# A two-branch layer (state-space scan beside dilated local attention) on one core: attention in natural token order

## The chip, the cores and the metric

One core of one Trainium2 chip runs the whole kernel. Times are device microseconds of one execution; the lower, the better. The core has five engines with an instruction stream each: PE (matrix products into PSUM), ACT and DVE (elementwise work and copies), POOL (small setup work) and SP (it only issues transfers). Transfers run on 16 DMA engines that SP and ACT feed through their queues.

## The reference

Two branches, each on its own x of 2048 tokens by 448, give 448 columns of the output each.

```
A: h[t] = Lam_bar * h[t-1] + B_bar @ x[t]          448 complex states, 2048 steps
   y[t] = 2 * Re(C @ h[t]) + x[t] * Dskip
B: q, k, v = split(x @ wqkv)                        16 heads of 28
   logits[t, w] = q[t] . k[t - 2w] * 28**-0.5       w = 0..7, masked where t - 2w < 0
   o[t] = sum_w softmax(logits)[t, w] * v[t - 2w]
   out_b = o @ wo
out = concat(y, out_b)                              bf16
```

## The kernel before

**Order of the work.** Python code describes the kernel as some 600 units (`Planner.add`), each with its engine, a cost, what it depends on and the buffers it takes. A list written out in the file, ORDER, then says in which order the units are emitted; each engine executes its share strictly in that order. So an instruction that waits holds everything behind it on its engine, and a transfer that waits holds SP. PSUM has two double banks (W) and four single ones (s).

**Branch B.** Token t = 16p + j lies in partition p, column group j. SP loads x transposed, one transfer per j (L348), and the weights of q, k and v (L326, L327). Projections (L466, L473, L499) give q and k transposed (channels on the partitions, qT, q3, kT, k3), a block of 8 j at a time, the upper block first. Logits: DVE multiplies q with k shifted by 2w tokens (`qk`, L639 to L645, 37 instructions in all), and PE sums each head's 28 channels with a selection matrix (L656, L662). Softmax (`softmax`, L684 to L716): maximum on DVE, exponential on ACT, sum on PE, reciprocal and normalising on DVE, transposes on PE, so that the weights lie with tokens on the partitions. V is projected for all 16 j (L741, four matmuls each) into `vd`, whose 14 leading slots are a halo: the slots of the previous partition. `halo` fills it by transfers inside the chip that shift by one partition, each cut in two, 112 partitions (L755) and 15 (L756); partition 0 is zeroed by POOL (L760). PV (`pv`): DVE multiplies weights and V (L797) and adds (L800, L809, L812), 3584 elements each; every group of four j adds to its own accumulator. The sums are transposed, for three of four groups by a transfer (L837), for the last on PE (L849), multiplied with wo (L866) and written out (L876).

**Branch A.** Parameters are turned into powers of Lam_bar on POOL and ACT (`setup`, its inputs loaded at L906 and transposed on PE at L988) and into small diagonal matrices on DVE (`powers`, L1146). The states go in seven groups m of 64 complex ones. For each, `scan` forms the input products (L1192, L1200), then a chain of PE products and ACT copies (eP L1205, e L1213, eG L1220, four steps through pbuf L1229 and L1234, h L1243, L1258, L1274); three groups are in flight. To finish a group its first values are added again with identity matmuls (L1252, L1263). `outputs` multiplies h with C (L1356) after adding x * Dskip by diagonal matmuls (L1353, six of eight pairs) or on DVE (L1367), copies (L1365) and writes out (L1370).

**The issue order on SP before the scan:** x of B, B matrices, x of A (L943, 16 transposes), halo, wo, C (L969, L973).

The lines of `halo` at issue:

```
def halo(i0, i1):
    f = lambda a, b, p0, p1: self.vd[p0:p1, a:b].rearrange("p j d h -> p (j d h)")
    s0, s1 = i0 + T, i1 + T
    nc.sync.dma_start(f(i0, i1, 1, 113), f(s0, s1, 0, 112))
    nc.sync.dma_start(f(i0, i1, 113, 128), f(s0, s1, 112, 127))
```

Of the kernel before, what the change touches and what calls it, by code (L numbers as in the profile page):

```python
# [9 lines left out]
ACT = mybir.ActivationFunctionType  # L10
# [18 lines left out]
TJ = HALO + T  # L29
# [3 lines left out]
JB = 8  # L33
QW = 2 + NCH
KPOW = [1, 2, 4, 8, 12, 16, 32, 48, 64, 128, 192, 256, 512, 768, 1024]
# [4 lines left out]
WARM = 4  # L40
FILL = (1, 3)
PRI = dict(bm=-5.66, xa=2.77, cc=19.9, sc=2.9, ch=-27.35, bk=-0.56, v0=16.0, v1=-26.16, wo=-13.74, y=14.16, pw=-5.68, sm=13.48, lim=100.0, lim2=30.0, limv=70.0, qk=0.86, K11=-14.0, Q11=-13.0, K10=-12.0, Q10=-11.0, K01=-10.0, Q01=-9.0, K00=-8.0, Q00=-7.0, d3=10.94, h0=-1.0, g0=-1.0, h1=-1.0, g1=-1.0, h2=-1.0, g2=-1.0, h3=1.0, g3=-1.0, h4=-1.0, g4=-1.0, h5=-1.0, g5=-1.0, h6=1.0, g6=1.0, nd=4.0, xd=20.12)
ORDER = [
# [51 lines left out]
class Unit:  # L95
    __slots__ = ("eng", "cost", "fn", "deps", "prio", "acq", "rel", "lat", "end", "seq", "on", "until", "mode")


class Planner:


    def __init__(self, bufs):
        self.units = []
        self.free = {k: [0.0] * n for k, n in bufs.items()}

    def add(self, eng, cost, fn, deps=(), prio=0.0, acq=None, rel=None, lat=None, until=None,
            mode="f"):
        u = Unit()
        u.mode = mode
        u.eng = eng if isinstance(eng, tuple) else (eng,)  # L110
        u.cost = cost if isinstance(cost, tuple) else (cost,)
        u.fn, u.prio, u.rel, u.until = fn, prio, rel, until
        u.acq = () if acq is None else (acq,) if isinstance(acq, str) else acq
# [4 lines left out]
        return u  # L118

    def run(self):  # L120
        left = list(self.units)
        nwait = {id(u): len({id(d) for d in u.deps}) for u in left}
        users = {}
        for u in left:
            for d in {id(d): d for d in u.deps}.values():
                users.setdefault(id(d), []).append(u)
        ready = [u for u in left if not nwait[id(u)]]
        clock = {}
        order = []
        n = len(left)  # L130
        mode = "f"
        while len(order) < n:
            best = None
            for u in ready:
                if any(len(self.free[a]) < u.acq.count(a) for a in u.acq):
                    continue
                for eng, cost in zip(u.eng, u.cost):
# [3 lines left out]
                    for a in u.acq:  # L141
                        t = max(t, sorted(self.free[a])[u.acq.count(a) - 1])
                    if u.until is not None and eng == u.eng[-1] and t > u.until:
                        continue
                    key = (t, u.prio, u.seq, t)
                    if best is None or key < best[0]:
                        best = (key, u, eng, cost + (0.095 if eng == "PE" and u.mode != mode else 0.0))
            assert best, "no unit can start: %d left, waiting for %s" % (n - len(order), [(u.acq, u.fn.__qualname__) for u in ready])
            (_, _, _, t), u, eng, cost = best
            for a in u.acq:  # L150
                self.free[a].remove(min(self.free[a]))
# [5 lines left out]
            for a in (u.rel,) if isinstance(u.rel, str) else u.rel or ():  # L157
                self.free[a].append(u.end)
# [5 lines left out]
            order.append((t, u, cost))  # L164
        self.order = order
        if len(ORDER) == n:
            for i in ORDER:
                u = self.units[i % 1000]
                u.on = u.eng[i // 1000]
                order.append((0.0, u, 0.0))  # L170
            order = order[n:]
        for _, u, _ in order:
            if len(u.eng) > 1:
                u.fn(u.on)
            else:
                u.fn()
# [15 lines left out]
class Ctx:  # L192
# [22 lines left out]
    def double(self, n, out, in_, deps, prio):  # L215

        return self.plan.add(("ACT", "DVE"), (act(n), vec2(n)), lambda eng: self.copy(eng, out, in_), deps, prio)
# [16 lines left out]
    def consts2(self):  # L234
# [19 lines left out]
        mrow = pool.tile([NCH, 4], bf16, name="mrow")  # L254
        mcol = pool.tile([NCH, 2, 2, NCH], bf16, name="mcol", tag="late_a")

        def masks():
            G.memset(mrow[:], 0.0)
            G.affine_select(out=mrow[:], in_=mrow[:], compare_op=ALU.not_equal, fill=-1e9,
                            base=-3, pattern=[[1, 4]], channel_multiplier=1)  # L260
            G.memset(mcol[:], 1.0)
            for b in range(2):
                for k in range(2):
                    v = mcol[:, b, k].rearrange("p (i r h) -> p i r h", i=4, r=2)
                    G.affine_select(out=v, in_=v, compare_op=ALU.is_ge, fill=0.0, base=8 * k - 8 * b - 1,
                                    pattern=[[-1, 4], [-4, 2], [0, H]], channel_multiplier=2)
        self.u_mask = self.plan.add("POOL", 2.7, masks, [self.boot], 1)

        def mask(b, lg):

            for k in range(2):
                nc.tensor.matmul(lg[:, 4 * k:4 * k + 4, 0], lhsT=mcol[:, b, 1 - k, :], rhs=mrow[:],
# [3 lines left out]
    def warm(self):  # L276

        nc, P = self.nc, self.plan
        self.pr = self.pool.tile([NCH, 3 * 4096], bf16, name="prods")
# [1207 lines left out]
```

## Time and profile before

| | |
|---|---|
| three runs | 141.4, 141.7, 141.99 us, median 141.7 |
| profiled execution, first to last instruction | 140.4 us |
| PE busy | 134.9 us in 1078 matmuls |
| DVE busy | 120.9 us in 128 instructions |
| ACT busy | 93.6 us in 182 instructions |
| granted clock of PE | 1.000 |
| DMA | 39390 packets, 15.99 MB |
| first q.k product on DVE | 15.48 us (half a unit), 21.98 us (the next) |
| last PV addition ends, last DVE instruction ends | 131.3 us, 137.9 us |

A row of groups reads: line, engine, operation, output<-inputs, sizes, count | busy us, mean ns of one | idle time before it and who ended it. A row of the order of time reads: start us, length us, engine, line, what. A row of the stage table reads: start:end, length, then busy us and count of PE, weight loads, DVE, ACT and POOL, then the granted clock, the mean busy share of the 16 DMA engines, and GB/s. "SPq" and "ACTq" are the issuing of transfers, whose data move later. The ends of matmuls are modelled, so two overlapping rows of PE give the pace by their starts.

### The profile page before, as it was taken

The numbers are of one execution on the slowest core, as the hardware profiler recorded it, in microseconds if no ns is written. First come the engines' busy times: TensorE is split into PE (matmuls) and PEld (weight loads), VectorE is DVE, ScalarE is ACT, GpSimd is POOL, SyncE is SP. The second block draws the span as 40 slices with busy tenths as digits, with TensorE's granted clock in tenths as the row PEclk, the third lists the DMA queues.
The fourth block names the chain that finished last, engine by engine and source line by source line (L and its number), as shares of the span: only waits on it lengthen the run. The fifth ranks groups of instructions, "written<-read, shape, count | busy, mean of one in ns | idle before, by whom it ended". The sixth has DMA issues, their size and how long they took to land.

```text
span 140.4 us, 2813 instructions
## 1 busy us (share of the span) xinstructions
PE 134.9 (96%) x1078; PEld 71.6 (51%) x1078; DVE 120.9 (86%) x128; ACT 93.6 (67%) x182; POOL 21.1 (15%) x68
## 2 busy tenths in 40 slices
PE   5999999999999999999999999999999999999990
PEld 1634333456554454666435554456655555555650
DVE  3245959999999989897998999999999999999931
ACT  3358879999765883578776789889873630551381
POOL 7374287000970000000000000000000000000000
PEclk9999999999999999999999999999999999999999
DMA  4965243996537616469999400600154155724044
GB/s 129 267 120 111 56 100 56 238 218 123 81 67 76 103 42 203 110 94 175 248 199 142 144 0 5 131 0 0 35 101 132 47 181 139 170 80 139 0 161 133
DMA packets 39390, 15.99 MB, mean 114 GB/s; under 512 B 31445, under 2 KB 38740, under 8 KB 39377
## 3 DMA queue, kind: packets, MB, share of 16 engines
q1 hardware_dynamic: 39314, 15.82, 50.6%
q8 instruction: 8, 0.13, 0.4%
q14 instruction: 5, 0.04, 0.1%
q10 hardware_dynamic: 63, 0.01, 0.0%
HBM read 4.27 MB, written 3.67 MB: 57 GB/s over the span
## 4 chain that ended last, share of the span: by engine, by line
PE 94%; DMA 2%; ACT 1%; issue 0%; DVE 0%; ACTq 0%
PE y_ps L1356 15%; PE qk_ps L466 12%; PE v_ps L741 9%; PE wo_ps L866 9%; PE scb L1192 7%; PE scP L1192 7%; PE logits L656 4%; PE scb L1234 3%; PE qk_ps L499 3%; PE qk_ps L473 2%; DMA ra<-in_B_x_dram 2%; PE scb L1209 2%; PE y_ps L1353 2%; PE scP L1200 2%; PE scP L1263 2%; PE pt_x L413 1%
## 5 line engine op out<-in xcount | busy, mean ns | idle before, releaser
L797 DVE TENSOR_TENSOR prods<-attn,vd 128x3584 bf16<-128x3584 bf16 x12 | 24.0, 2020 | 0.0
L641 DVE TENSOR_TENSOR prods<-qk 128x3072 bf16<-128x3072 bf16 (+1 forms) x17 | 22.8, 1379 | 1.0 <-PE logits L656 0.5
L800 DVE TENSOR_TENSOR rb<-rb,prods 128x3584 bf16<-128x3584 bf16 x11 | 22.2, 2022 | 0.1
L466 PE MATMUL qk_ps<-rb 128*128 128x512 bf16 x60 | 15.3, 386 | 0.0
L1356 PE MATMUL y_ps<-Ccat,qk 128*128 128x448 bf16 x64 | 14.9, 352 | 0.0
L866 PE MATMUL wo_ps<-wo_p,rb 128*128 128x448 bf16 x64 | 13.5, 352 | 0.0
L741 PE MATMUL v_ps<-rb 128*128 128x448 bf16 x64 | 13.1, 352 | 0.0
L1229 ACT CAST pbuf<-scb 128x128 bf16<-128x128 f32 x35 | 9.2, 272 | 4.9 <-PE scb L1234 4.3
L1192 PEld LDWEIGHTS <-Bcat 128*128 128x128 bf16 x84 | 7.6, 98 | 8.2 <-issue 1.9
L1356 PE MATMUL y_ps<-Ccat,h 128*128 128x448 bf16 x48 | 11.7, 353 | 0.0
L1365 ACT CAST qk<-y_ps 128x896 bf16<-128x896 f32 x6 | 5.4, 907 | 9.1 <-PE y_ps L1356 9.1
L201 ACT CAST qk<-wo_ps 128x448 bf16<-128x448 f32 (+1 forms) x16 | 8.3, 526 | 4.2 <-PE wo_ps L866 3.9
L1192 PE MATMUL scb<-xaT_sb,Bcat 128*128 128x512 bf16 x42 | 11.1, 380 | 0.0
L1192 PE MATMUL scP<-xaT_sb,Bcat 128*128 128x512 bf16 x42 | 10.9, 379 | 0.0
L201 ACT CAST qk<-qk_ps 128x512 bf16<-128x512 f32 (+2 forms) x14 | 7.8, 580 | 2.9 <-PE qk_ps L473 1.2
L203 ACT ACTIVATE qk<-qk_ps 128x512 bf16<-128x512 f32 (+1 forms) x16 | 9.3, 599 | 0.5 <-PE qk_ps L499 0.2
L466 PEld LDWEIGHTS <-rb 128*128 128x128 bf16 x60 | 5.8, 100 | 7.4 <-issue 1.2
L201 ACT CAST vd<-v_ps 128x448 bf16<-128x448 f32 x16 | 7.9, 542 | 2.5 <-PE v_ps L741 2.5
L1356 PEld LDWEIGHTS <-qk 128*128 128x128 bf16 x64 | 6.3, 98 | 5.8
L645 DVE TENSOR_TENSOR prods<-qk 128x768 bf16<-128x768 bf16 (+3 forms) x18 | 9.1, 569 | 0.1
L741 PEld LDWEIGHTS <-rb 128*128 128x128 bf16 x64 | 6.1, 98 | 5.3
L866 PEld LDWEIGHTS <-rb 128*128 128x128 bf16 x64 | 6.1, 98 | 5.0
(177 smaller groups left out, 251.9 us busy)
## 6 DMA issues: line engine op xcount, KB each, us to landing
out_dram<-qk SPq DMA_DIRECT2D x18, 112.0 KB, 1.7
out_dram<-qk SPq DMA_DIRECT2D x7, 224.0 KB, 2.2
vd<-vd SPq DMA_DIRECT2D x3, 392.0 KB
rb<-in_B_wqkv_dram SPq DMA_DIRECT2D x3, 336.0 KB
qk<-in_A_x_dram SPq DMA_DIRECT2D x1, 448.0 KB
ra<-in_A_B_re_dram SPq DMA_DIRECT2D x1, 392.0 KB
ra<-in_A_B_im_dram SPq DMA_DIRECT2D x1, 392.0 KB
rb<-in_A_C_re_dram SPq DMA_DIRECT2D x4, 98.0 KB
```

The source lines that it names most:

```text
L201: nc.scalar.copy(out, in_)
L203: nc.scalar.mul(out, in_, scale)
L466: nc.tensor.matmul(out(n), lhsT=w(n, full, k), rhs=self.xT[:, j:j + 4, k, :], start=(not rfirst and k == 1), stop=(rfirst and k == KT - 1) ...
L641: V.tensor_tensor(out.rearrange("p i j k q -> p i (j k) q"), qq.unsqueeze(1).to_broadcast([NCH, 2, 4 * nk, NCH]), bass.AP(kk.tensor, kk.of ...
L645: V.tensor_tensor(jk(out[:, i, a:e]), qq, kk, op=ALU.mult)
L741: nc.tensor.matmul(ps[:].rearrange("p h d -> p (h d)"), lhsT=self.xT[:, j, k, :], rhs=self.wv[:, k, :], start=(k == 0), stop=(k == KT - 1))
L797: V.tensor_tensor(tmp[i].rearrange("p (j d h) -> p j d h", j=8, d=DH), aa, self.vd[:, o:o + 8], op=ALU.mult)
L800: V.tensor_tensor(acc, acc, tmp[i], op=ALU.add)
L866: nc.tensor.matmul(ps[:], lhsT=o[:, kt, :], rhs=self.wo_p[:, KT * e + kt, :], start=(kt == 0), stop=(kt == KT - 1))
L1192: mt(box[i], lhsT=self.Bcat[:, k, m, :], rhs=self.xk(slice(i, None, 4), k), start=(i % 2 == 0 and k == 0), stop=False, **kw)
L1229: nc.scalar.copy(pb[:, dst, PAD:], box[3][:, 384:512])
L1356: nc.tensor.matmul(ps, lhsT=self.h[m][:, i, g * NCH:(g + 1) * NCH], rhs=self.Ccat[:, m, :], start=(m == 0 and not skip), stop=(m == NM - 1 ...
```

## The change

- **Tokens.** Branch B works on two halves of 1024 tokens, t = 1024b + 8p + j, first half first. x comes as pairs of tokens, 896 channels in seven blocks of 128: eight transposing transfers instead of thirteen. The q and k weights are loaded by ACT's queue, ahead of the parameters of branch A, in an even and an odd layout of seven blocks (the middle one is shared, half each).
- **Matmuls.** Each projection of q, k and V is three full matmuls and one half-row matmul per token of the pair; the two half-row ones are emitted together and work on different halves of PE's rows. The scan's loading is unchanged in this.
- **q.k products.** q and k lie in token order, so one instruction of 4096 elements covers four shifts of one half: 7 per half, 14 in all. k3 and q3 get their second copy by two transfers on SP. The sums in PE have 512 columns instead of 256.
- **Softmax.** The reciprocal is a logarithm and an exponential on ACT. The transposed weights go to DRAM and come back in the order in which V lies (`away`, `move`); then ACT or DVE turns them (`turn`).
- **V and PV.** Each half has its own V buffer of 22 slots, 14 of them halo. A shift by one partition is one transfer of 127 partitions, a shift by two one of 126; the second half also fetches the first half's last partitions. PV uses instructions of 7168 elements: two products and one addition per group of four j, then folds.
- **Scan.** The steps through pbuf are five on 64 columns instead of four on 128. The first values are put back by ACT copies into PSUM instead of identity matmuls, except where the bank is held (groups 3 and 6). h of groups 3 to 6 lies where the first half's V was; ACT's copy of it waits for the last PV product of that half.
- **Skip.** x is loaded again in token order over its transposed copy once the scan's input products are done, multiplied by Dskip on DVE (four instructions of 1792), and copied by ACT into PSUM before the y matmuls.
- Eight warm-up matmuls stand before the first projection instead of four; the ORDER list is a new one, and a second list names the PSUM banks.

```diff
-            nc.sync.dma_start(f(i0, i1, 1, 113), f(s0, s1, 0, 112))
-            nc.sync.dma_start(f(i0, i1, 113, 128), f(s0, s1, 112, 127))
...
+            def halo(i0, i1, b=b):
+                n = 2 if i0 < HALO - JB else 1
+                s0 = i0 + JB * n
+                nc.sync.dma_start(flat(b, n, NCH, i0, i1), flat(b, 0, NCH - n, s0, s0 + i1 - i0))
+                if b:
+                    nc.sync.dma_start(flat(1, 0, n, i0, i1), flat(0, NCH - n, NCH, s0, s0 + i1 - i0))
+            for i0, i1 in ((6, 10), (10, 14), (0, 6)):
...
+        def away():
+            d = box["d"] = cx.dram.tile([8, NCH, NCH], bf16, name="attn_d%d" % b)
+            nc.sync.dma_start(d[:].rearrange("g q e -> q g e"), self.at)
+
+        def move():
+            nc.sync.dma_start(self.at, box["d"][:].rearrange("g (p j) e -> (g p) j e", j=JB))
...
+                    V.tensor_tensor(p, q[:, t0:t0 + HB].unsqueeze(1).to_broadcast([NCH, 4, HB]),
+                                    bass.AP(k.tensor, k.offset, [k.ap[0], [DIL, 4], [1, HB]]), op=ALU.mult)
...
+                def rr(mm=mm):
+                    mm(0, lo, 3)
+                    mm(1, hi, 3)
...
+                if eng == "ACT":
+                    nc.scalar.copy(box[1], box["e1"][:])
...
-                for k in range(KT if skip and m0 == 0 else 0):
-                    n = min(NCH, D - k * NCH)
-                    nc.tensor.matmul(ps[:, k * NCH:k * NCH + n], lhsT=self.xk(j + jj, k), rhs=self.Dg[:, k, 0:n],
-                                     start=(k == 0), stop=False, skip_group_check=True)
...
+            def seed(j=j, jb=jb):
+                jb["y"] = self.psum.tile([NCH, 2, 512], f32, name="y_ps", slot=jb["s"])
+                nc.scalar.copy(jb["y"][:, :, 0:D], self.xd[j])
...
-    b.qk(1, PRI["qk"])
-    b.qk(0, PRI["qk"] + 1)
...
+    b.qk(0, PRI["qk"])
+    b.qk(1, PRI["qk"] + 1)
```

The instructions of the changed kernel around the halo stand on SP in this order: the 16 transposes of branch A's x, the second copies of k3 and q3, halo slots 6 to 9 (127 partitions), the wo loads, slots 10 to 13 (127), the skip row, `away` of the first half, slots 0 to 5 (126), `move` of the first half, slots 6 to 9 of the second half, and later, behind C's loads and the second half's `away`, its slots 0 to 5, its slots 10 to 13, `move` and C's transpose.

More of the change, by code (lines that the diff above doesn't have):

```diff
@@ L215, in double @@
     def double(self, n, out, in_, deps, prio):
-        return self.plan.add(("ACT", "DVE"), (act(n), vec2(n)), lambda eng: self.copy(eng, out, in_), deps, prio)
+        return self.plan.add(("ACT", "DVE"), (act(n) + 0.04, vec2(n)), lambda eng: self.copy(eng, out, in_), deps, prio)
     def consts(self):
@@ L286, in mm @@
             if first:
-                box["ps"] = self.psum.tile([NCH, 2, 512], f32, name="warm_ps", tag="W")
+                box["ps"] = self.psum.tile([NCH, 2, 512], f32, name="warm_ps", slot=self.warm_slot)
             for _ in range(n):
@@ L648, in summ @@
                     if head:
-                        self.lg[b] = self.psum.tile([NCH, W, NCH], f32, name="logits", tag="W")
+                        self.lg[b] = self.psum.tile([NCH, W, NCH], f32, name="logits", slot=self.lg_slot[b])
                     lg, pr = self.lg[b], ub["pr"]
-                    new = tp // 2 not in begun
-                    begun.add(tp // 2)
-                    zs = slice(H - H * par, 3 * H - H * par)
-                    for kt in range(3):
-                        for i in range(4):
-                            nc.tensor.matmul(lg[32 * i:32 * i + 32, 2 * tp:2 * tp + 2, :],
-                                             lhsT=cx.Z[:, kt, zs], rhs=pr[:, :, i, kt, :],
-                                             start=(new and kt == 0), stop=(kt == 2), skip_group_check=True)
@@ L727, in v_proj @@
+        u = P.add("PE", pe(8, 128), tr, [u], -1, acq=s_at, rel="at")
+        u = P.add("ACT", act(1024), ev, [u, *self.u_attn.get(0, ())], -1, rel=s_at)
+        u = P.add("SP", 0.6, away, [u], -1, lat=2.3)
+        u = P.add("SP", 0.6, move, [u], -1, lat=2.3)
+        self.u_attn[b] = [P.add(("ACT", "DVE"), (act(512), vec2(512)), lambda eng, r=r: turn(eng, r), [u], -1) for r in range(2)]
     def v_proj(self, prio, deps):
-        nc, pool, P, cx = self.nc, self.pool, self.plan, self.cx
+        nc, P, cx = self.nc, self.plan, self.cx
@@ L839, in pv @@
-        for j in range(j0, j0 + JB):
-            jb = {}
-            g = j // 4
-            def tr(j=j, jb=jb):
-                pt = jb["pt"] = self.psum.tile([NCH, KT, NCH], f32, name="pt_o", tag="s")
+                    o = (3584, 6272, 8064)[g]
+                    t = self.oTd[g] = rb[:, o:o + n1].rearrange("p (k q) -> p k q", q=NCH)
+                    nc.sync.dma_start(t, res[g], transpose=True)
+                trs[r] = self.u_trd[g] = P.add("SP", 2.5, trd, [lasts[r][1], *self.u_vm], PRI["wo"], lat=2.0)
@@ L845, in tr @@
+        for j in range(JB):
+            jb, st, sl = {}, Slot("s", 2), Slot("s", 1)
+            g = 2 * b + j // 4
+            def tr(j=j, jb=jb, st=st):
+                pt = jb["pt"] = self.psum.tile([NCH, KT, NCH], f32, name="pt_o", slot=st)
                 a = j % 4 * D
@@ L1260, in back @@
-            def back(box=box):
-                box["P"] = self.psum.tile([NCH, 2, 512], f32, name="scP", tag="W")
-                for i in range(2):
-                    mt(box["P"][:, i, :], lhsT=cx.ident[:], rhs=box["eP"][:, i, :], start=True, stop=False, **kw)
-            def s6(box=box, pb=pb, L=L, hget=hget):
-                carry(box["P"][:, 0, :], L(1), pb, hget())
-            def s7(box=box, L=L, hget=hget):
-                mt(box["P"][:, 1, :], lhsT=L(1), rhs=hget()[:, 1, :], start=False, stop=True, **kw)
@@ new lines, in s5, with ev1f @@
+            def s5(box=box, L=L, hget=hget, carry=carry, sl=sl, m1=m1):
+                if m1 == "add":
+                    box[1] = self.psum.tile([NCH, 512], f32, name="scb1", slot=sl["b1"])[:]
+                carry(box[1], L(2), hget(), m1 == "add")
+            def ev1f(eng, box=box, hget=hget, m1=m1):
+                if m1 == "add":
+                    nc.vector.tensor_tensor(hget()[:, 1, :], box[1], box["e1"][:], op=ALU.add)
+                else:
+                    cx.copy(eng, hget()[:, 1, :], box[1])
@@ new lines, in back, with p2 @@
+            def back(eng, box=box, sl=sl, mP=mP):
+                box["P"] = self.psum.tile([NCH, 2, 512], f32, name="scP", slot=sl["P2"])
+                if eng == "ACT":
+                    nc.scalar.copy(box["P"][:], box["eP"][:])
+                else:
+                    for i in range(2):
+                        mt(box["P"][:, i, :], lhsT=cx.ident[:], rhs=box["eP"][:, i, :], start=True, stop=False, **kw)
+            def p2(box=box, sl=sl, mP=mP):
+                if mP == "add" and "P2" not in box:
+                    box["P"] = box["P2"] = self.psum.tile([NCH, 2, 512], f32, name="scP", slot=sl["P2"])
+                return box["P"]
@@ L1396 @@
+                P.add("SP", 0.1, lambda f=out: f(j0=1, j1=2), [v, o], pr, rel="ya", lat=2.0)
 @with_exitstack
```

1108 lines of the change are left out of this document (487 added, 621 removed), and 59 rows, old and new, of tables (BANKS, ORDER).

## Prediction

> **What bounds the kernel now.** I read the page's busy shares and its chain first, then busy time by stage, then the groups by shape, then the order of time on each queue.
>
> ```profile
> span 140.4 us, 2813 instructions
> PE 134.9 (96%) x1078; PEld 71.6 (51%) x1078; DVE 120.9 (86%) x128; ACT 93.6 (67%) x182; POOL 21.1 (15%) x68
> ...
> PE 94%; DMA 2%; ACT 1%; issue 0%; DVE 0%; ACTq 0%
> ```
> ```profile
> 20.00:25.00 5.00, 5.00 (x24) 2.06 (x23) 4.52 (x6) 4.37 (x9) 3.80 (x8) 1.00 0.33 66
> ...
> 80.00:90.00 10.00, 10.00 (x70) 5.11 (x67) 9.93 (x7) 8.95 (x20) 0.00 (x0) 1.00 0.24 46
> ...
> 120.00:130.00 10.00, 10.00 (x61) 5.34 (x60) 9.96 (x6) 3.57 (x6) 0.00 (x0) 1.00 0.43 123
> ```
> In the stage rows (length, then busy us of PE, PEld, DVE, ACT, POOL, then clock, DMA share, GB/s) PE is full throughout and DVE is full from about 22 us on. The chain names PE, but shortening PE alone would not carry far: DVE stands right beside it. So the new time is the later of two chains: DVE (first q.k product, then DVE's work and its waits, then a tail) and the scan on ACT and PE with the y products behind it.
>
> **PE: about 6 us less.** The pace of a matmul is read from the chain.
> ```profile
> 34.90 3.78 PE v_ps L741 x20
> ...
> 90.53 0.32 PE scP L1200 x2
> 90.85 0.22 PE scb L1200 x2
> ...
> 131.44 0.89 PE pt_o L849 x16
> ```
> ```profile
> L1353 PE MATMUL y_ps<-Dg,xaT_sb 128*128 128x128 bf16 (+1 forms) x48 | 4.3, 212 | 0.0
> ...
> L1263 PE MATMUL scP<-eP,ident 128*128 128x512 bf16 x10 | 3.0, 378 | 0.0
> ...
> L1252 PE MATMUL scb<-e,ident 128*128 128x512 bf16 x6 | 2.3, 378 | 0.0
> ```
> 448 columns take 0.189 us, 128 take 0.056; a pair of half-row matmuls runs side by side in 0.22, plus 0.1 to enter that mode. Gone are the 48 skip matmuls (about 48 x 0.055 = 2.6) and the 16 identity matmuls (16 x 0.22 = 3.5). V goes from 64 full matmuls to 48 and 8 pairs: 8 x 0.189 = 1.5 less, 8 x 2 x 0.1 = 1.6 more. The projections go from 88 and 12 pairs to 98 of 512 columns, the logits keep their columns: 0.4 less, nothing. The scan's middle goes from 10 to 11 narrower matmuls per group: nothing. Sum about -6.5 us.
>
> **ACT: about 20 us more, not the bound by itself.**
> ```profile
> L1229 ACT CAST pbuf<-scb 128x128 bf16<-128x128 f32 x35 | 9.2, 272 | 4.9 <-PE scb L1234 4.3 <-PE scb L1226 0.2
> ...
> L1205 ACT CAST eP<-scP 128x1024 bf16<-128x1024 f32 x7 | 7.2, 1028 | 1.5 <-PE scP L1200 1.4
> ...
> L1213 ACT CAST e<-scb 128x512 bf16<-128x512 f32 x7 | 4.2, 595 | 2.4 <-PE scb L1209 2.4
> ```
> ACT now writes PSUM before the matmuls add to it: 5 x 1.03 and 6 x 0.6 in the scan, 8 x 0.91 before y, 16.3 in all, and one more short copy per group, 7 x 0.27. A write of ACT into PSUM is not in this trace: between nothing extra and twice the eviction of that size, I take the eviction's time. 93.6 + 18 + a few evictions is under 115.
>
> **DVE: about the same work, begun 7 us earlier.**
> ```profile
> L797 DVE TENSOR_TENSOR prods<-attn,vd 128x3584 bf16<-128x3584 bf16 x12 | 24.0, 2020 | 0.0
> L800 DVE TENSOR_TENSOR rb<-rb,prods 128x3584 bf16<-128x3584 bf16 x11 | 22.2, 2022 | 0.1
> L641 DVE TENSOR_TENSOR prods<-qk 128x3072 bf16<-128x3072 bf16 x11 | 19.2, 1757 | 1.0 <-PE logits L656 0.5 <-ACT vd L201 0.2
> ```
> ```profile
> 21.98 1.76 DVE L641 TENSOR_TENSOR prods<-qk 128x3072 bf16<-128x3072 bf16 x1
> 23.65 1.06 DVE L639 TENSOR_TENSOR prods<-qk 128x1536 bf16<-128x1536 bf16 x1
> ...
> 129.24 2.09 DVE L812 TENSOR_TENSOR rb<-rb,prods 128x1792 bf16<-128x1792 bf16 x2
> ```
> The step from 3072 to 3584 elements is 263 ns, 0.51 ns each, and the next instruction starts some 0.09 us before the record ends (21.98 to 23.65). So a product of 4096 costs 2.2 us and a PV instruction of 7168 3.8. Along the new DVE order: up to the copy that turns the first half's attention, 14 x 2.2 + 4 x 1.07 (powers) + 0.5 + 2.3 + 1.2 + 1.5 (the wait for the last logits) = 40.6. From there to the same copy of the second half: 4 x 3.8 + 2 x 3.85 + 2 x 3.1 + 3 x 1.07 + 2 = 34.3. Then to the end of PV, with four skip multiplications of 1.1 instead of one: 4 x 3.8 + 2 x 3.85 + 3.1 + 4.3 + 2.1 + 1.4 = 33.8. The tail after PV is taken from this run: 140.4 - 131.3 = 9.1.
>
> The first product starts later than the loads alone would allow:
> ```profile
> 0.81 0.58 ACTq L906 DMA_DIRECT2D prm<-in_A_Lambda_re_dram  x1
> ...
> 2.82 0.58 SPq L326 DMA_DIRECT2D rb<-in_B_wqkv_dram  x1
> 3.44 0.49 SPq L327 DMA_DIRECT2D rb<-in_B_wqkv_dram  x1
> ...
> 3.98 10.45 SPq L348 DMA_TRANSPOSE rb<-in_B_x_dram  x8
> ```
> ```profile
> 86.68 1.53 SPq L837 DMA_TRANSPOSE rb<-rb  x1
> ```
> ```profile
> 1.26 1.89 PE L289 MATMUL warm_ps<-prods 128*128 128x512 bf16 x4 [1.26 <-DVE prods L282]
> ```
> A transpose of four blocks holds SP for 1.31 us, one of 14 (L837) for 1.53, so one of seven is priced at 1.31 and the first four of x leave SP by 6 us. The three parameter loads now stand behind eight weight loads on ACT's queue, eleven issues of about 0.5 with 2.2 to land, and their transpose is ahead of every projection on PE: about 8.4. Then 4.2 us of projections, 1.2 of eviction, 0.5 of handing over: 14.3, against 21.98 now. The warm-up matmuls run at 0.42 us, half the later pace. The Trainium skill ("TensorE: Matmul & The Clock Gate", Part 1) says that PE falls back to half clock after an idle window of about 3.4 us. By it PE, idle from 4.7 to 8.4, would pay about 2 us again; the sum leaves this out.
>
> **The copy of V's halo, the term that decides.** Each halo slot is V shifted by one partition. Today a copy of 127 partitions is cut in two, 112 (L755) and 15 (L756). The new one moves 127 in a single transfer, twice in the first half of PV and twice in the second.
> ```profile
> L755 SPq DMA_DIRECT2D vd<-vd x4: 547/588/893, 51.5 to 67.6; - x4
> L756 SPq DMA_DIRECT2D vd<-vd x4: 817/902/1420, 52.2 to 68.5; - x4
> ...
> DMA to landing us min/median/max: 2.2/3.4/4.6
> ```
> ```profile
> 54.30:56.00 1.70, 1.70 (x9) 0.78 (x8) 1.53 (x3) 0.59 (x1) 0.00 (x0) 1.00 0.91 267
> ...
> 66.60:67.40 0.80, 0.80 (x6) 0.25 (x3) 0.80 (x2) 0.76 (x2) 0.00 (x0) 1.00 0.92 346
> ```
> How an odd count is dealt to the 16 engines is not shown, so two ends: spread as today's pair, landing in 3.4 us; or all on one engine. There one engine moves 346 / (0.92 x 16) = 23.5 GB/s in the halo's own stretch (18.3 in the other), and 127 rows of 3584 B, 455 KB, take 19.4 us (24.9). 112 is 7 x 16; 127 divides by nothing. The nearer row is the 15: a seventh of the data, yet its issue takes 902 ns against 588, so the row count does change how a transfer is made. I take one engine, 19.4.
>
> The Trainium skill ("DMA: Bandwidth & Descriptors", "Why a DMA increments its semaphore by 16 and not by 1") says that a transfer uses the largest count up to 16 that divides its slowest dimension, and names 127 partitions as one engine. By it the time is the 172 below, by the even spread 137; no run here shows it.
>
> When: SP issues 25 transposes and the loads between them first.
> ```profile
> 29.27 8.67 SPq L943 DMA_TRANSPOSE xaT_sb<-in_A_x_dram  x6
> ```
> 8 x 1.31, 17 x 1.45 and some 12 plain issues of 0.6, with a wait for the first k3 copy, put the first 127-row copy at 44.5 and its data at 45.5 to 64.9; the second runs behind it to 84.3. Behind both on the same engine stands a share of every later transfer, the first half's attention on its way to DRAM and back among them:
> ```profile
> out_dram<-qk SPq DMA_DIRECT2D x18, 112.0 KB, 1.7
> out_dram<-qk SPq DMA_DIRECT2D x7, 224.0 KB, 2.2
> ```
> The trip is two transfers of 256 KB, the second issued only when the first has landed (SP waits, and what stands behind it on SP waits too). By the rows of 112 and 224 KB I take 2.1 each: back at 88.5. DVE stands at the turning copy from 14.3 + 40.6 = 54.9. Spread, the trip would return at about 57.
>
> **Sum, against this execution's 140.4.** 88.5 + 34.3 = 122.8; the second pair is issued near 86 and 113 and ends between 123 and 134, so 0 to 11 more, I take 5; + 33.8 + 9.1 = 170.7. Beside it, ACT's copy of scan group 3 waits for the last first-half product (88.5 + 24.7, the part of the 34.3 up to it, = 113.2; the copy overwrites that V); then three groups of ACT work at 7.3 (22), 112 y matmuls, 8 x 4 wo matmuls and 32 transposes (21.2 + 6.0 + 1.8 = 29), 3.3 to the end: 167.5. The median of the runs, 141.7, lies 1.3 over this span, so I forecast 172.
>
> **Rivals.** (1) One engine, but later transfers are not held back: the readers of the halo alone wait, the second product until 84.3, then 30.2 (the 34.3 without the turning copy and the first product), 4 for the fourth copy (84.3 + 2 x 19.4 = 123.1, 4 after its reader would be ready), 33.8, 9.1: 161.4, with the 1.3 about 163. For it: engines off the backlog go on. Against: every transfer of SP is on one queue. (2) The other sign: the 127 rows are spread. Then DVE's chain is 57 + 34.3 + 33.8 + 9.1 = 134.2 and the scan's 81.7 + 22 + 29 + 3.3 = 136; with the 1.3 137, faster. It decides if a copy lands within about 8 us: at that point the gains above are used up. (3) The DRAM trip proves slow by itself (10 us and more): it adds to either case, and alone brings (2) to no change.
>
> **Chances.** One engine with the queue held 0.44, rival 1 0.30, rival 2 0.23, rival 3 cancelling the gain 0.03. Faster or slower means by over 0.5%, about what a measurement of this kernel can tell: faster 0.23, same 0.02, slower 0.75. The likeliest case alone spans 160 to 184 (rates of 23.5 and 18.3, second wait 0 to 11). The range takes in rival 1 and half of rival 2: 136 to 182.
>
> **What would show it.** Right: DVE idle for 25 to 35 us near 55 to 90, released by a transfer; DMA share near one sixteenth there; landings of 127-row copies of 18 to 40 us; ACT and PE idle in the same stretch. Wrong: landings of 3 to 5 us and a gap at 55 of a few us. The start is right if the first product begins at 13 to 16, PE if it is busy near 128 us in all, DVE if its products take 2.28 us and PV's 3.9. A PV instruction far over 3.9, or ACT over 115 busy, would break the sum in either case.

## The result, and the profile after

The changed kernel takes 205.7 us (median of four runs, 204.9 to 206.4) where the kernel before takes 141.7: 1.450 times as long, 95% interval 1.446 to 1.455. I had forecast 172 with a range of 136 to 182. The direction was right and the size was wrong. Some executions of the three edited kernels of experiment 1 took 2 to 5% longer than the fastest of the same kernel; the times given for them leave these out (one of four, three of four and three of six remain), and their traces are of longer ones (157.9, 203.8 and 154.0 us).

The head of the page of the changed kernel, with the shares of its chain by engine:

```profile
span 203.2 us, 2449 instructions
PE 133.7 (66%) x916; PEld 68.6 (34%) x916; DVE 114.9 (57%) x79; ACT 104.6 (51%) x194; POOL 28.6 (14%) x66
...
PE 39%; DMA 25%; DVE 13%; SPq 9%; ACT 6%; POOL 4%; issue 2%; ACTq 0%; DVEq 0%; POOLq 0%
```

Work explains little: PE and DVE are busy for a little less than before, POOL for 7.5 us more and ACT for 11. The span grew by 62.8 us because they all wait. The chain, which was PE for 94%, is now for a third transfers and their issuing (DMA 25%, SPq 9%). DVE's part of the order of time shows where:

```profile
26.69 9.41 DVE L532 TENSOR_TENSOR prods<-qk 128x4096 bf16<-128x4096 bf16 x4
...
102.95 0.29 DVE L243 COPY ra<-ra 128x512 bf16<-128x512 bf16 x1 [32.39 <-DMA ra<-attn_d]
...
155.38 0.29 DVE L243 COPY ra<-ra 128x512 bf16<-128x512 bf16 x1 [16.42 <-DMA ra<-attn_d]
```

The first product begins at 26.7, and DVE stands still for 32.4 and for 16.4 us before the two copies that turn the attention on its return from DRAM. SP's part of the same view shows why the attention is late (L668 are the halo copies, L599 the way to DRAM, L602 the way back, L670 the few rows that the second half fetches from the first):

```profile
55.91 0.74 SPq L668 DMA_DIRECT2D ra<-ra  x1
56.71 21.03 SPq L412 DMA_DIRECT2D wo_p<-in_B_wo_dram  x8
77.84 0.64 SPq L668 DMA_DIRECT2D ra<-ra  x1
78.58 7.12 SPq L1233 DMA_DIRECT2D rb<-in_A_Dskip_dram  x1
85.80 0.97 SPq L599 DMA_DIRECT2D attn_d<-ra  x1
...
100.20 0.34 SPq L602 DMA_DIRECT2D ra<-attn_d  x1
...
133.63 7.98 SPq L670 DMA_DIRECT2D qk<-ra  x1
141.72 0.55 SPq L602 DMA_DIRECT2D ra<-attn_d  x1
```

Right behind the first copy of 127 rows the eight small loads of wo, 0.48 us each in the kernel before (3.83 for eight), hold SP for 21 us. The first of them takes 7.7 us to issue. The eighth then waits 8.5 us until the copy has landed, at 77.4:

```profile
SPq L412 <- DMA ra<-ra: 8.5, 1, 8.5
```

It waits because each transfer reports its landing, one count for the share of each DMA engine that carries it, to one of eight counters, which the transfers of SP and ACT use by turns; in the trace a transfer is issued only when the one before it on its counter has landed. The first half's attention leaves at 85.8, its 256 KB reach DRAM at 100.2, 14.4 us later. The stage rows of that time (length, then PE, PEld, DVE, ACT, POOL busy, granted clock, DMA share, GB/s):

```profile
70.00:75.00 5.00, 5.00 (x31) 2.39 (x30) 0.56 (x1) 4.31 (x8) 0.00 (x0) 1.00 0.06 25
80.00:85.00 5.00, 5.00 (x43) 2.67 (x40) 0.00 (x0) 4.70 (x15) 0.00 (x0) 1.00 0.06 22
90.00:95.00 5.00, 0.00 (x0) 0.00 (x0) 0.00 (x0) 0.00 (x0) 0.00 (x0) 0.54 0.06 27
```

The DMA share is 0.06, one engine in sixteen, at 22 to 27 GB/s. That is the picture that the prediction gave for one engine.

The late start is a second matter. ACT's issues, PE's first work and the stage row of that time:

```profile
10.30 0.54 ACTq L808 DMA_DIRECT2D prm<-in_A_Lambda_re_dram  x1
14.76 0.31 ACTq L808 DMA_DIRECT2D prm<-in_A_Lambda_im_dram  x1
15.11 0.30 ACTq L808 DMA_DIRECT2D prm<-in_A_log_dt_dram  x1
```
```profile
18.52 0.17 PE L882 MATMUL pp<-ident,prm 21*128 21x21 bf16 x1 [13.66 <-DMA prm<-in_A_log_dt_dram]
18.62 9.30 PE L451 MATMUL qk_ps<-rb 128*128 128x256 bf16 x66
```
```profile
5.00:15.00 10.00, 0.00 (x0) 0.00 (x0) 0.00 (x0) 0.00 (x0) 0.00 (x0) 0.68 1.19 252
```

From 5 to 15 us no engine computes and the DMA engines are full. Eleven issues on ACT, priced at half a microsecond each, took until 15.4, because ACT stood between them.

### The profile page after: what moved, and what is told of

The parts are those of the page before. It is cut to its first block, busy times and chain, and to the rows that moved or that the text cites. A ratio compares the mean times of both kernels' runs of the same rounds, so it can differ in the third digit from the quotient of the medians.

```text
span 203.2 us, 2449 instructions
## 1 busy us (share of the span) xinstructions
PE 133.7 (66%) x916; PEld 68.6 (34%) x916; DVE 114.9 (57%) x79; ACT 104.6 (51%) x194; POOL 28.6 (14%) x66
## 3 DMA queue, kind: packets, MB, share of 16 engines
HBM read 6.89 MB, written 4.19 MB: 55 GB/s over the span
## 4 chain that ended last, share of the span: by engine, by line
PE 39%; DMA 25%; DVE 13%; SPq 9%; ACT 6%; POOL 4%; issue 2%; ACTq 0%; DVEq 0%; POOLq 0%
PE y_ps L1259 10%; DMA ra<-attn_d 8%; DMA attn_d<-ra 7%; PE wo_ps L768 6%; DMA rb<-rb 5%; PE qk_ps L451 5%; DVE prods L698 4%; SPq L670 4%; SPq L379 4%; DVE prods L532 4%; DMA rb<-in_B_x_dram 3%; PE v_ps L643 3%; PE logits L545 3%; PE scb L1078 2%; PE scP L1078 2%; DVE prods L704 2%
## 5 line engine op out<-in xcount | busy, mean ns | idle before, releaser
L768 PE MATMUL wo_ps<-wo_p,rb 128*128 128x448 bf16 x64 | 16.4, 395 | 29.0 <-DMA rb<-rb 29.0
L532 DVE TENSOR_TENSOR prods<-qk 128x4096 bf16<-128x4096 bf16 x14 | 32.3, 2353 | 1.2 <-PE logits L545 0.6
L451 PE MATMUL qk_ps<-rb 128*128 128x256 bf16 (+2 forms) x132 | 23.0, 340 | 0.0
L768 PEld LDWEIGHTS <-rb 128*128 128x128 bf16 x64 | 6.4, 107 | 34.7 <-DMA rb<-rb 29.5
L704 DVE TENSOR_TENSOR prods<-prods 128x7168 bf16<-128x7168 bf16 x4 | 15.5, 3886 | 0.0
L698 DVE TENSOR_TENSOR prods<-ra 128x7168 bf16<-128x7168 bf16 x4 | 15.4, 3886 | 0.3 <-DVE ra L243 0.3
L698 DVE TENSOR_TENSOR prods<-ra,qk 128x7168 bf16<-128x7168 bf16 x4 | 15.5, 3887 | 0.0
L1259 PE MATMUL y_ps<-Ccat,ra 128*128 128x448 bf16 x64 | 15.0, 352 | 0.0
L643 PE MATMUL v_ps<-wv,rb 128*128 128x448 bf16 (+1 forms) x64 | 14.8, 371 | 0.1
L451 PEld LDWEIGHTS <-rb 128*128 128x128 bf16 (+1 forms) x132 | 12.1, 104 | 7.0 <-issue 2.1
L1078 PE MATMUL scP<-xaT_sb,Bcat 128*128 128x512 bf16 (+1 forms) x56 | 14.2, 391 | 0.2 <-ACT ra L239 0.2
L1078 PE MATMUL scb<-xaT_sb,Bcat 128*128 128x512 bf16 (+1 forms) x56 | 14.1, 383 | 0.0
L643 PEld LDWEIGHTS <-rb 128*128 128x128 bf16 (+1 forms) x64 | 5.2, 99 | 23.7 <-issue 19.9
```

The costliest lines, as they stand in the source:

```text
L451: nc.tensor.matmul(out(e)[:, j0:j1], lhsT=w, rhs=self.xB[rows, b, j0:j1, c, :], start=e not in begun, stop=True, skip_group_check=True)
L532: V.tensor_tensor(p, q[:, t0:t0 + HB].unsqueeze(1).to_broadcast([NCH, 4, HB]), bass.AP(k.tensor, k.offset, [k.ap[0], [DIL, 4], [1, HB]]), ...
L643: nc.tensor.matmul(box[e][:].rearrange("p h d -> p (h d)"), lhsT=self.xB[rows, b, jj, c, :], rhs=self.wv[rows, c, :], start=e not in begun ...
L698: V.tensor_tensor(out.rearrange("p (u i d h) -> p u i d h", u=4, i=4, d=DH), self.attn[b][:, r].rearrange("p (x u i) h -> p x u i h", x=2, ...
L704: V.tensor_tensor(T1, T1, T2, op=ALU.add)
L768: nc.tensor.matmul(ps[:], lhsT=o[:, kt, :], rhs=self.wo_p[:, KT * e + kt, :], start=(kt == 0), stop=(kt == KT - 1))
```

## The experiments

**1. The halo copies cut, the parameters loaded first, and the one copy merged in the old kernel.** Three edits, the first two also together:

```diff
-                nc.sync.dma_start(flat(b, n, NCH, i0, i1), flat(b, 0, NCH - n, s0, s0 + i1 - i0))
+                for p0, p1 in ((0, 112), (112, NCH - n)) if n == 1 else ((0, NCH - n),):
+                    nc.sync.dma_start(flat(b, n + p0, n + p1, i0, i1), flat(b, p0, p1, s0, s0 + i1 - i0))
```

> The changed kernel with each 127-row halo copy cut in 112 rows and 15 rows (four copies; the 126-row ones stay). One-engine theory: DVE's two waits for the attention's way through DRAM, 32.4 and 16.4 us, go (0 to 3 left in all), SP's issues of the wo loads fall from 21 us to about 4, and the time is 205.7 - 48.8 = 157 (153 to 163). Rival, the trip through DRAM is slow by itself: both waits stay at about 14, 180 or more. Rival, the copies were spread already: 205.

Measured: 154.4 us, 51.3 less. The way of the attention, and the landing of the cut copies (ns of each issue, then us to landing):

```profile
64.96 0.40 SPq L599 DMA_DIRECT2D attn_d<-ra  x1
65.40 0.83 SPq L669 DMA_DIRECT2D ra<-ra  x1
68.59 0.34 SPq L602 DMA_DIRECT2D ra<-attn_d  x1
```
```profile
L669 SPq DMA_DIRECT2D ra<-ra x5: 557/835/947, 55.6 to 65.4; - x5
...
DMA to landing us min/median/max: 3.3/3.4/3.5
```

The way to DRAM takes 3.6 us instead of 14.4, DVE's first wait shrinks to 2.05 and its second goes. Both waits came from the one line of code that makes 127 partitions one transfer; a slow DRAM trip as such is excluded.

```diff
-    b.loads()
-    a.loads_params()
+    a.loads_params()
+    b.loads()
```

> The changed kernel with the three parameter loads issued ahead of the eight weight loads on ACT's queue, nothing else. If the parameter transpose at the head of PE's order is what delays the start, PE's projections begin at 10 to 13 instead of 18.6, the first product at 19 to 21 instead of 26.7, and the copies leave SP some 5 earlier: 200 (198 to 202). If the start is bound by the bytes in flight (x and weights), the first product stays within 1.5 us of 26.7 and the time within 1%.

Measured: 200.0 us, ratio to the kernel before 1.410 (1.405 to 1.416). The time fits, the mechanism only in part: in its trace, of 203.8 us, projections began at 8.5, but the first product at 23.45, 3.2 earlier and not 6, because PE waited for weights in between. How the 5.7 us of gain arise is not shown.

> Both edits. If they are two separate costs, 157 - 6 = 151 (146 to 156), still slower than the 141.7 of the kernel before; if the start is bound by bytes, 157. The term that would then be left of my sum is the tail after the start: about 125 us from first product to the end where I had 122.

Measured: 150.1 us (1.059, 1.055 to 1.063), 4.3 less than with the cut alone: the two are separate costs. The first product stands at 25.50 in its trace.

In the kernel before, the reverse edit:

```diff
-            nc.sync.dma_start(f(i0, i1, 1, 113), f(s0, s1, 0, 112))
-            nc.sync.dma_start(f(i0, i1, 113, 128), f(s0, s1, 112, 127))
+            nc.sync.dma_start(f(i0, i1, 1, 128), f(s0, s1, 0, 127))
```

> The kernel before with its four halo copies each made as one transfer of 127 rows instead of 112 and 15. One-engine theory: 3.5 times 19.4 us in a row on one engine from 51.5 on, the last at about 119, where the product that reads it stood at about 90: 175 (165 to 190). If row counts do not matter: 141 to 142.

Measured: 188.9 us (1.334, 1.329 to 1.339). One DVE row carries it, and one of SP shows how far the hold reaches, C's transpose, 4.19 us of SP before:

```profile
126.29 2.03 DVE L796 TENSOR_TENSOR prods<-attn,vd 128x3584 bf16<-128x3584 bf16 x1 [46.66 <-DMA vd<-vd]
```
```profile
96.41 30.57 SPq L972 DMA_TRANSPOSE Ccat<-rb  x1
```

Nothing else of the change is needed for the loss: the merged copy alone costs the old kernel 47 us.

**2. The copy by itself.** A chain of fourteen copies between two tiles, one line each, so that an issue waits for the landing of the copy ahead.

```
nc.sync.dma_start(a[1:128], b[0:127])      # L57
nc.sync.dma_start(b[1:127], a[0:126])      # L58
nc.sync.dma_start(a[1:125], b[0:124])      # L59
...
nc.sync.dma_start(a[1:114], b[0:113])      # L63
nc.sync.dma_start(b[1:113], a[0:112])      # L64
```

> The copy alone: fourteen copies between two tiles, rows of 3584 B shifted by one partition, each issued when the one ahead has landed, with 128, 127, 126, 124, 121, 120, 119, 113, 112, 96, 64, 63, 15 and again 127 rows (all of the reference's work is left out; the time beside the kernel before says nothing). If a transfer goes on as many engines as the largest number up to 16 that divides its row count (16, 1, 14, 4, 11, 15, 7, 1, 16, 16, 16, 9, 15, 1) and one engine moves a row in 0.15 us, then above a fixed part of some 2 us the data take 1.2, 19.4, 1.4, 4.7, 1.7, 1.2, 2.6, 17.2, 1.1, 0.9, 0.6, 1.1, 0.2 and 19.4 us. If every count that 16 does not divide goes on one engine: 126, 124, 121, 120 and 119 take 18 to 19 as well, and 63 takes 10. If 127 rows are slow only beside other traffic: all about 3.5.

```profile
2.76 0.56 SPq L56 DMA_DIRECT2D b<-a  x1
5.60 0.72 SPq L57 DMA_DIRECT2D a<-b  x1
25.96 0.85 SPq L58 DMA_DIRECT2D b<-a  x1
29.57 0.63 SPq L59 DMA_DIRECT2D a<-b  x1
38.53 0.79 SPq L60 DMA_DIRECT2D b<-a  x1
...
53.54 0.65 SPq L63 DMA_DIRECT2D a<-b  x1
71.95 0.57 SPq L64 DMA_DIRECT2D b<-a  x1
75.43 0.54 SPq L65 DMA_DIRECT2D a<-b  x1
```
```profile
7.00:25.50 18.50, 3.20 (x1) 0.00 (x0) 1.00 0.06 24
```

From one issue to the next, in us:

| rows | 128 | 127 | 126 | 124 | 121 | 120 | 119 | 113 | 112 | 96 | 64 | 63 | 15 |
|---|---|---|---|---|---|---|---|---|---|---|---|---|---|
| largest divisor up to 16 | 16 | 1 | 14 | 4 | 11 | 15 | 7 | 1 | 16 | 16 | 16 | 9 | 15 |
| us | 2.8 | 20.4 | 3.6 | 9.0 | 5.0 | 4.1 | 5.9 | 18.4 | 3.5 | 3.2 | 2.8 | 3.5 | 2.5 |

One row more on one engine costs (20.36 - 18.41) / 14 = 0.139 us, which leaves 20.36 - 127 x 0.139 = 2.7 fixed. The count of rows decides, not their bytes: 126 rows take less than a fifth of the time of 127. It is the largest divisor up to 16 that sets the number of engines; a rule by multiples of 16 would have put 126, 121 and 63 with 127. Only 124 is off: 31 rows on each of four engines would be 7.0 and took 9.0. By the completion counts, which come one from each engine, two of the four were done after 7.2 us and two only after 8.9; why is open.

The Trainium skill ("DMA: Bandwidth & Descriptors", "Why a DMA increments its semaphore by 16 and not by 1") states just this rule and names 127 partitions as one engine. This run agrees, 20.4 us against 3.6 for 126.

**3. Held by the queue or by the engine?** The two transfers of each attention half go to ACT's queue; the halo stays on SP's.

```diff
-            nc.sync.dma_start(d[:].rearrange("g q e -> q g e"), self.at)
+            nc.scalar.dma_start(d[:].rearrange("g q e -> q g e"), self.at)
...
-            nc.sync.dma_start(self.at, box["d"][:].rearrange("g (p j) e -> (g p) j e", j=JB))
+            nc.scalar.dma_start(self.at, box["d"][:].rearrange("g (p j) e -> (g p) j e", j=JB))
```

> The changed kernel, its 127-row copies as they are, with only the two transfers of each attention half (to DRAM and back) issued by ACT instead of SP. If the copies hold back only what stands behind them on SP's own queue, the first half is back near 73 instead of 103, its second product then waits for the second copy (about 97), the 16.4 us of the second half shrink to 0 to 8, and the time is about 188 (182 to 196). If the one engine serves all queues in order of issue, nothing changes: 204 to 206.

Measured: 214.2 us (1.511 to the kernel before, 1.506 to 1.517), slower than either theory had. ACT's rows:

```profile
64.23 0.21 ACT L1117 CAST pbuf<-scb 128x64 bf16<-128x64 f32 x1
77.77 0.40 ACTq L599 DMA_DIRECT2D attn_d<-ra  x1
78.21 0.21 ACT L1117 CAST pbuf<-scb 128x64 bf16<-128x64 f32 x1 [13.77 <-DMA wo_p<-in_B_wo_dram]
...
92.69 0.36 ACTq L602 DMA_DIRECT2D ra<-attn_d  x1
```

ACT was free at 64.4 and issued only at 77.8. The row behind it names what it waited for, a load of wo. It is the transfer ahead of ACT's on the same counter, the third of the eight loads; fifteen of its sixteen shares had landed by 66.8, and the last, on the copy's engine, at 77.70. The issue itself then took 0.40 us, and the next one on ACT 0.36 us with the second copy under way, so the copies do not hold back the issuing on ACT's queue as such. On SP's queue the transfer right behind a copy does take long to issue: 7.7 us for the first load of wo, 8.0 for L670 above. Why is open.

The data then took 14.9 us, against 14.4 on SP's queue: fifteen shares had landed by 81.1, the sixteenth at 92.67. The Trainium skill ("DMA: Bandwidth & Descriptors", "Issuing engines are not separate DMA queues") says that transfers of all issuers run on the same 16 engines; the 14.9 us agree. The order differs a little: from ACT's queue the data landed 7.6 us ahead of the second copy (100.27), and from SP's queue at 100.18, 0.8 behind it (99.37). So neither theory had it right: another queue does not free a transfer of the copy, and the one engine does not serve both queues strictly in order of issue. The first half's attention was back 4.4 us earlier than in the changed kernel (98.57), yet the kernel took 8.5 us longer. ACT, which computes, now stands where SP stood, for 13.8 us here and for 10.2 at the way back; that this is what costs the time is likely, but was not separated.

**4. One pair at a time.** The cut of experiment 1 for the first half of PV only, then for the second only (`b == 1`).

```diff
-                for p0, p1 in ((0, 112), (112, NCH - n)) if n == 1 else ((0, NCH - n),):
+                for p0, p1 in ((0, 112), (112, NCH - n)) if n == 1 and b == 0 else ((0, NCH - n),):
```

> The changed kernel with the 127-row copies cut only in the first half of PV (two of the four). If each pair costs by itself what DVE waits for it, the 32.4 us before the first half go and some 16 stay: 174 (171 to 179). If one pair is enough to hold everything back, most of it stays: over 190.

> The changed kernel with the 127-row copies cut only in the second half of PV, the counterpart of the run with the first half cut (188.1). No cut gave 205.7, both cut 157.7. If the waits that DVE shows in the changed kernel are prices of their own, this is 205.7 - 16.4 = 189. If the pairs' prices add up (17.6 and 30.4), it is 175. If the first pair alone costs as much as the second did alone, 188.

Measured: 188.1 us with the first pair cut (expected 174), 186.4 with the second cut. Against 154.4 with both cut, the second pair alone costs 33.7 us, the first alone 32.0, both together 51.3. (The expectation above reckons with 157.7 for both cut, and so with 30.4 for the second pair.) The waits of the two kernels, the first pair cut, then the second:

```profile
DVE ra L243 <- DMA ra<-attn_d: 17.4, 2, 16.2
...
DVE qk L243 <- PE wo_ps L769: 16.3, 2, 15.8
```
```profile
DVE ra L243 <- DMA ra<-attn_d: 32.0, 1, 32.0
```

In each of these kernels the price is what DVE waits for there: 17.4 + 16.3 = 33.7, and 32.0. It is not what DVE waits for in the changed kernel, where the second pair shows only 16.4. With the first wait gone, the transpose that the first wo products need is issued 9.3 us behind the third copy (94.23 and 84.89) and holds SP for 11.6 us, 3.0 of them for its input; in the changed kernel it comes 18.7 us behind that copy and holds SP for 2.3. DVE gets a wait of 15.8 us that the changed kernel does not have. So a wait in one profile is not the price of its cause in another kernel: in the changed kernel the first pair's wait hid half of the second pair's.

**5. The start.** Q's weights are taken from ACT's queue and issued on SP between x's first four blocks and its last four (on top of both edits of experiment 1).

```diff
-            wload(nc.scalar, c0, odd)
+            if kind == "K":
+                wload(nc.scalar, c0, odd)
...
+            if (b, j) == (0, 1):
+                wload(nc.sync, 0, 0)
+                wload(nc.sync, 0, 1)
```

> The cut copies and the early parameter loads, and in addition Q's weights issued on SP between x's first four blocks and its last four, instead of on ACT's queue beside all eight. If the first product waits for the bytes issued ahead of it (3.4 MB by 21 us), taking 0.9 MB from in front moves the last Q weight from 21 to 16 to 17, the first product from 25.5 to 20 to 21.5, and the time from 151.7 to 147 (145 to 149). If the start is bound by the count of transposes or by PE's cold clock, less than 1.5 us moves.

Measured: 149.15 us (1.053, 1.049 to 1.057), the best complete version, but only 0.9 us below the 150.1 of the kernel without this edit, less than their intervals can tell apart, where 147 was expected. The first product did move:

```profile
18.19 9.41 DVE L536 TENSOR_TENSOR prods<-qk 128x4096 bf16<-128x4096 bf16 x4
```

It comes 8.5 us earlier than in the changed kernel (26.69): the order in which the same transfers are issued sets the start. How much of it the parameters bring and how much the weights is not shown. (The 7.3 and 2.6 us in the next expectation are counted from 25.50 and 151.75.) The end hardly moved, so something behind the start sets it. The chain of waits of this kernel names the place, the transpose of the first half's second result:

```profile
100.65 5.64 DMA rb<-rb
106.34 1.67 PE wo_ps L773 x4
```

The 5.64 us are the transfer's; PE itself stood 2.7 us for it.

**6. Where the earlier start goes.** On SP that transpose stands behind C's transpose of 28 blocks. First it goes ahead of it, with two loads of x for the skip term, by an edit of ORDER alone (258 is that transpose, 248 is C's, 558, 562, 560 and 556 are the loads; 486 is a unit of PE in between):

```diff
-    197, ... 248, ... 486, ... 558, ... 258, ... 562, ... 560, ... 556
+    197, ... 486, 258, 558, 562, 248, ... 560, ... 556
```

> The last kernel (cut copies, early parameter loads, Q's weights ahead of x's second half) with one more edit: on SP the transpose of the first half's second result and two loads of x for the skip term are issued ahead of C's transpose of 28 blocks instead of behind it. There the first product came 7.3 us earlier and the end only 2.6; PE stood 5.6 us before the wo products that wait for that transpose, and the scan's last steps stood behind them. If that place took the gain, the transpose lands at 101 to 102 instead of 106.3, DVE's wait of 3.4 before its last PV addition shrinks to under 1, and the time is 145.5 (144 to 147.5). If the end is set by PE's own work or by DVE, it stays within 1 us of 149.

Measured: 149.95 us (1.056, 1.052 to 1.061), no gain. DVE's wait before the last addition fell from 3.4 to 0.2 as expected; in its place

```profile
DVE xaT_sb L1248 <- DMA xaT_sb<-in_A_x_dram: 5.2, 3, 2.2
```

Then all four loads go ahead:

```diff
-    197, ... 486, 258, 558, 562, 248, ... 560, ... 556
+    197, ... 486, 258, 558, 562, 560, 556, 248
```

> As the last reordered kernel, but all four loads of x for the skip term go ahead of C's transpose on SP, where two went before. There the wait ahead of the wo products was gone and the time did not move: DVE stood 1.69, 2.20 and 1.33 us before its skip multiplications instead, for loads that C's transpose held back. If that is the whole story, these waits fall below 1 us in all, the last PV addition ends at about 134.5 instead of 139.2, and the time is 145.5 (144.5 to 147.5), still above 141.7. If PE's y and wo products set the end by now, it stays at 149 to 150.

Measured: 151.8 us (1.071, 1.064 to 1.078), worse. Those waits are down to 1.2, and now the y products wait for C:

```profile
DVE prods L719 <- PE pt_o L757: 5.2, 1, 5.2
PEld L1265 <- DMA Ccat<-rb: 4.8, 1, 4.8
```

So no order serves all three. The last run takes one of them away:

```diff
-            nc.sync.dma_start(self.Ccat[:].rearrange("p m (a q) -> p (m a) q", q=KP),
-                              self.cn2[:].rearrange("p m a r q -> p (m a r q)"), transpose=True)
+            nc.gpsimd.memset(self.Ccat[:], 0.0)
```

> The kernel with cut copies, early parameter loads and Q's weights ahead of x's second half (149.15), with C's transpose of 28 blocks left out: its tile is filled with zeros by POOL instead (the y products run on zeros). That transpose holds SP for 4.4 us at 95.5, between the trip of the second attention half and the transposes and loads that PE and DVE wait for next. If it is what took back the gain of the earlier start, PE's 5.6 us before the wo products, DVE's waits for x's loads (1.9) and its 3.4 before the last PV addition all shrink together, and the time is 144.5 (143 to 146.5). If PE's and DVE's own work sets the end, it stays at 148 to 149.5.

Measured: 146.05 us (1.030, 1.023 to 1.036), at the upper part of what was expected, and all three waits are under 1 us. C's transpose, left out here, is worth 3.1 us to the kernel of experiment 5; the other transfers beside it on SP were only put in another order. In the kernel before, C's transpose left SP at 70.4, long before anything like this:

```profile
70.44 4.19 SPq L973 DMA_TRANSPOSE Ccat<-rb  x1
```

In the changed kernel C is loaded into the place where x stood, and so only after V's products. No version here beats the kernel before; the best complete one is 5.3% slower.

## Why the prediction was right in kind and wrong in size

**The term that decides: right.** One engine for 127 rows, 19.4 us for the data; the copy alone takes 20.4 with everything. That a share of every later transfer is held: right. Of the sixteen shares of each of the first seven loads of wo fifteen had landed by 66 to 70.5 us, and the last landed at 77.6 to 78.8, right behind the copy (77.4). What I did not have is that transfers of the other queue wait as well, through the counters (experiment 3). Rival 1, in which only the readers wait, is refuted by the first wait of DVE, which is for the attention, and by these landings; rival 2, spread copies, by experiment 2; rival 3, a slow DRAM trip, by experiment 1 (3.6 us to DRAM, against 2.1 taken).

**The sum: wrong by 32.5 us of span (203.2 against 170.7).** By its own steps:

| step | predicted | measured |
|---|---|---|
| first product | 14.3 | 26.7 |
| first 127-row copy issued | 44.5 | 55.9 |
| first half's attention back | 88.5 | 102.95 |
| from there to the second turn | 34.3 + 5 | 52.4 |
| from there to the end of PV | 33.8 | 38.3 |
| tail | 9.1 | 9.5 |

Two terms failed. The first is the start: "eleven issues of about 0.5 with 2.2 to land" took the issues as free of waits. Six of them stood until an earlier transfer with the same counter had landed, among them the one at 10.30 for a weight load issued at 4.11 (landed 10.28) and the one at 14.76 for a transpose of x issued by SP at 8.65 (landed 14.74). With the DMA engines at a share of 1.19 these two took about 6 us to land and not 2.2. I priced the new queue by its issue times alone. It put SP's list of transfers, the copies among them, 11.4 us later, and that is most of the 14.5 by which the attention came back late. The second is "0 to 11 more, I take 5" for the second pair: DVE waits 16.4 there. I let its two copies overlap work of PV; but the way back of the second half (L602, 141.7) stands behind the fourth copy (132.3) on the same path as in the first half, and I did not put the same mechanism to it twice: the way back landed at 155.35, right behind that copy (154.68). So the second pair took 13.1 us more than the 39.3 of that step. Experiment 4 prices that pair, alone, at 33.7. The rest of the 32.5 is smaller: 3.0 in the first pair and the trip, 4.5 from the second turn to the end of PV, 0.4 in the tail; these were not followed further. The range, built from the same two terms, was too narrow for the same reason.

**PE, -6.5 us.** Not seen in the changed kernel (133.7 busy) and seen in part where the stalls are gone (130.4 in the kernel of experiment 5, -4.5). In the stalls the granted clock falls, 0.54 in the row above at 90 to 95. The Trainium skill ("TensorE: Matmul & The Clock Gate", Part 1) gives half clock after an idle window; the 0.68 of the row from 5 to 15 agrees in kind. Its price at the start was not separated.

**ACT and DVE: right.** The groups by shape in the changed kernel:

```profile
L532 DVE TENSOR_TENSOR prods<-qk 128x4096 bf16<-128x4096 bf16 x14 | 32.3, 2353 | 1.2 <-PE logits L545 0.6 <-ACT qk L241 0.4
...
L698 DVE TENSOR_TENSOR prods<-ra 128x7168 bf16<-128x7168 bf16 x4 | 15.4, 3886 | 0.3 <-DVE ra L243 0.3
```
```profile
L1271 ACT CAST y_ps<-xaT_sb 128x896 f32<-128x896 bf16 x8 | 7.3, 913 | 0.2
L1091 ACT CAST eP<-scP 128x1024 bf16<-128x1024 f32 x7 | 7.1, 1018 | 0.6 <-PE scP L1078 0.6
...
L1160 ACT CAST scP<-eP 128x1024 f32<-128x1024 bf16 x5 | 5.1, 1028 | 0.0
```

Products 2.35 (2.28 said), PV 3.89 (3.9 said), ACT 104.6 busy (under 115 said). ACT's writes into PSUM cost what the eviction of that size costs, 1.03 and 0.91, the value taken. (The 16.3 for these writes in the sum should read 16.0.)

**The side forecast of rival 2, 137 without the stall, was too good as well.** In the last run the blocks are, from the first product: 45.4, 34.7, 35.2 and a tail of 9.8, where I had 40.6, 34.3, 33.8 and 9.1. The first block is 4.8 longer, 4.4 of it in small waits (POOL's input to the diagonal matrices 1.6, the attention's trip 1.5, three waits for PE and ACT of 0.3 to 0.6), and it begins at 19.7 and not 14.3. With the other blocks this makes 12.6, which is 144.7 against the 132.1 of my terms. A sum of durations along one engine's order leaves out such waits, and a gain of a few per cent is of their size.

## What to carry to other kernels

Look at the row count of every transfer inside the chip before anything else: a count whose largest divisor up to 16 is small goes on that few engines, 127 rows in 20.4 us where 112 and 15 land in 3.4, and a later transfer is late by the share that falls to such an engine, with everything that waits for it, whichever queue it is on. Price a start by when the transfers ahead of the first result land, not by issue times alone, once the DMA share is near 1. And do not read a wait in the profile as the price of its cause in another kernel: two waits of 32 and 16 us had prices of 32 and 34 alone, and 51 together; apply a mechanism at every place where its pattern occurs.

## What the runs showed of the hardware that I had not expected

A transfer on one DMA engine can hold up an engine that neither issued it nor reads it: ACT waited 13.3 us (64.4 to 77.8) to issue one transfer, because the load of wo ahead of it on its counter had its last share behind the copy. C's transpose, 4.19 us of SP in the kernel before, took 30.57 behind two merged copies. And four engines did not all finish together: of the 124 rows two engines were done after 7.2 us, the time that follows from the row time, and two after 8.9.
